# The 128-byte start of SBUF tiles in a channel-attention and Gelu feed-forward kernel

## The chip, the cores and the metric

One core of a Trainium2 chip runs the whole program. The metric is the device time of one execution in microseconds (us), the median of several executions. A time ending in ns is in nanoseconds.

## The reference, cut to what matters

```
q, k, v: (4, 6080, 256) float32; tau: a number; w_in: (256, 2048); w_out: (2048, 256)
qn = q / (norm(q over the 6080 rows) + 1e-6);  kn likewise
s  = kn^T @ qn / tau                 # 256 x 256 for each of the 4 batches
a  = softmax(s), each row divided by (its sum + 1e-9)
x  = v @ a                           # (24320, 256)
out = gelu(x @ w_in) @ w_out
```

## The kernel before, in words

Products are made in float32r, each operand split into a high part and a low remainder, so that one product is three matmuls (high by high, high by low, low by high). Attention is folded into the weights: for each batch the softmax matrix (`eh`, `el`) is multiplied into `w_in` by `w_group` (lines 341 to 364), which leaves the tiles `wh` and `wl`. The main loop then takes `v` in pairs of column blocks, 512 columns each (480 in the last of six pairs of a batch), and for each pair runs eight units. A unit is 7 first products (`product`, lines 416 to 418: weights `wh`/`wl`, moving operand `vh`/`vl`), Gelu on ScalarE (lines 424, 425), the split of its result (line 426), and 8 second products (lines 486 to 488: weights `wo`, moving operand `gh`/`gl`): 21 + 24 = 45 matmuls. There are 4 x 6 x 8 = 192 units.

Beside the units the next batch is prepared. `burst` (lines 177, 179) adds up its 256 x 256 score matrix out of `hl`: pairs of one 512-column matmul, whose moving operand is two runs of 256 columns, and one 256-column matmul. `norm_part` (lines 198, 199) loads `k` and `q` transposed and squares them on ScalarE, 24 activations a batch, each with its sum in a column of `nsum`. `softmax` (lines 264 to 335) is a generator of some stages: the sum of `nsum` (`nx`, line 281), its root on ScalarE (`ny`, 288), VectorE arithmetic (`nz`, `nr`, lines 291 to 294), `diag` and `rk` (297, 300), a matmul (303), the scaling and the row maximum (306, 309), the exponential with its sum in `den` (316), and `rden` (318, 319). Batch 0 does its part before the main loop with plain float32 matmuls (line 142), and its softmax stands alone on the way to the first unit.

A scheduler of the framework orders each engine's instructions: what is ready may be moved ahead of what was written earlier. A tile of a pool is used again only when the last instruction on its former holder is through; the pool `pm`, where all of the softmax's tiles lie, has one buffer for each name. A wait inside a tile goes by the slice that is read or written.

Tiles lie in SBUF one behind the other, pool by pool, each size rounded up to 32 bytes, at the same address in all partitions. In the kernel before the starts are, as remainders of 128 bytes:

| tiles | start mod 128 |
|---|---|
| `ident`, `ones`, `wh0` to `wh3`, `wl0` to `wl3` | 0 |
| `taut`, `rtau` (4 bytes each, the last of `const`) | 0, 32 |
| `win`, `wo`, `raw`, `hl`, `kqc`, `v_raw`, `vs`, `vh`, `vl`, `osb` | 64 |
| `junk`, `nx` | 64, 96 |
| `t0`, `t1` | 0 |
| `diag` | 96 |
| `e0`, `e1` | 64, 32 |
| `eh`, `el`, `sacc`, `nsum` (96 bytes) | 0 |
| `p1`, `p5`, `u2`, `h`, `gh`, `g`, `gl`, and in the first stage `raw0`, `acc`, `acc_p`, `sq` | 96 |

Of the kernel before, what the change touches and what calls it, by code (L numbers as in the profile page):

```python
# [9 lines left out]
F32 = mybir.dt.float32  # L10
F32R = mybir.dt.float32r
U32 = mybir.dt.uint32
AF = mybir.ActivationFunctionType
ALU = mybir.AluOpType
AX = mybir.AxisListType

P = 128
# [5 lines left out]
NCT = C // P  # L23
# [28 lines left out]
def channel_attention_gelu_ffn(ctx, tc, qk, kqt, vt, tau, w_in, w_out, out):  # L52
# [10 lines left out]
    nc = tc.nc  # L63
    const = ctx.enter_context(tc.tile_pool(name="const", bufs=1))
# [4 lines left out]
    pm = ctx.enter_context(tc.tile_pool(name="pm", bufs=1))  # L69
# [5 lines left out]
    def f32(ap):  # L75
        return ap.bitcast(F32)
# [6 lines left out]
    state = {}  # L83
# [10 lines left out]
    def bank():  # L94
        return ps_h.tile([P, NT], F32, name="ph")
# [4 lines left out]
    def load_first(js):  # L100
        if js % 3 == 2:
            raw = pqk.tile([P, JS, 2, C], F32, name="raw", bufs=3)
        else:
            raw = pst.tile([P, JS, 2, C], F32, name="raw0", bufs=4)
        step = 1 if js == 0 else JS
        for j in range(0, JS, step):
            nc.sync.dma_start(out=raw[:, j:j + step], in_=qk[0, :, js * JS + j:js * JS + j + step])
        raws[0, js] = raw
# [47 lines left out]
    def sum_up(nps, acc, start, stop):  # L156
        for i in range(2 * NCT):
            nc.tensor.matmul(nps[:, i:i + 1], acc[:, i // NCT, i % NCT * P:(i % NCT + 1) * P],
                             ones[:, 0:1], start=(start and i == 0), stop=stop, skip_group_check=True)
# [29 lines left out]
    NSC = -(-N // NS)  # L189

    def norm_part(b, i):

        t, c = divmod(i, NSC)
        n = min(NS, N - c * NS)
        if i == 0:
            state["nsum"] = pm.tile([P, 2 * NCT, NSC], F32, name="nsum")
        x = pqk.tile([P, NS], F32, name="kqc", bufs=2)
        nc.sync.dma_start(out=x[:, :n], in_=kqt[b, t, :, c * NS:c * NS + n])
        nc.scalar.activation(out=x[:, :n], in_=x[:, :n], func=AF.Square,  # L199
                             accum_out=state["nsum"][:, t, c:c + 1])  # L200
# [57 lines left out]

    def preload(func, after):

        junk = pm.tile([P, 2], F32, name="junk")
        nc.scalar.activation(out=junk, in_=after.bitcast(F32)[:, 0:2], func=func)

    def softmax(first, pool, name):
        x = pm.tile([P, 2 * NCT], F32, name="nx")
        ts = []
        for m in range(NCT):
            t = pm.tile([P, C], F32, name=f"t{m}")
            if first:
                nc.scalar.copy(out=t, in_=state["s"][m])  # L270
            else:
                s = state["sacc"]
                nc.vector.tensor_tensor(out=t, in0=s[:, m, 0:C], in1=s[:, m, C:2 * C], op=ALU.add)
            ts.append(t)
        if first:
            nps, acc = state.pop("nps"), state.pop("acc")
            for j in range(JS):
                sum_up(nps, acc[:, j], False, j == JS - 1)
            nc.vector.tensor_scalar(out=x, in0=nps[:, 0:2 * NCT], scalar1=1e-30, scalar2=None, op0=ALU.max)
        else:  # L280
            nc.vector.reduce_sum(out=x, in_=state["nsum"], axis=AX.X)
            nc.vector.tensor_scalar(out=x, in0=x, scalar1=1e-30, scalar2=None, op0=ALU.max)
        yield

        y = pm.tile([P, 2 * NCT], F32, name="ny")
        z = pm.tile([P, 2 * NCT], F32, name="nz")
        r = pm.tile([P, 2 * NCT], F32, name="nr")
        nc.scalar.activation(out=y, in_=x, func=AF.Sqrt)
        if first:
            preload(AF.Exp, y)  # L290
        nc.vector.reciprocal(out=z, in_=y)
        nc.vector.tensor_tensor(out=z, in0=z, in1=x, op=ALU.mult)
        nc.vector.scalar_tensor_tensor(out=z, in0=z, scalar=2e-6, in1=y, op0=ALU.add, op1=ALU.add)
        nc.vector.reciprocal(out=r, in_=z)

        diag = pm.tile([P, NCT, P], F32, name="diag")
        nc.vector.tensor_tensor(out=diag, in0=ident.unsqueeze(1).broadcast_to([P, NCT, P]),
                                in1=r[:, NCT:2 * NCT].unsqueeze(2).broadcast_to([P, NCT, P]), op=ALU.mult)
        rk = pm.tile([P, NCT], F32, name="rk")
        nc.vector.tensor_scalar(out=rk, in0=r[:, 0:NCT], scalar1=rtau, scalar2=4.0, op0=ALU.mult, op1=ALU.mult)  # L300
        yield
        rq = pool.tile([P, NT], F32, name=name)
        nc.tensor.matmul(rq[:, 0:C], ones, diag.rearrange("p h d -> p (h d)"), start=True, stop=True)
        nms = []
        for m in range(NCT):
            nc.vector.scalar_tensor_tensor(out=ts[m], in0=ts[m], scalar=rk[:, m:m + 1], in1=rq[:, 0:C],
                                           op0=ALU.mult, op1=ALU.mult)
            nm = pm.tile([P, 1], F32, name=f"nm{m}")
            nc.vector.reduce_max(out=nm, in_=ts[m], axis=AX.X, negate=True)
            nms.append(nm)  # L310
        yield
        es, rs = [], []
        for m in range(NCT):
            e = pm.tile([P, C], F32, name=f"e{m}")
            den = pm.tile([P, 1], F32, name=f"den{m}")
            nc.scalar.activation(out=e, in_=ts[m], func=AF.Exp, bias=nms[m], accum_out=den)
            rden = pm.tile([P, 1], F32, name=f"rden{m}", bufs=2)
            nc.vector.tensor_scalar(out=den, in0=den, scalar1=1e-9, scalar2=None, op0=ALU.add)
            nc.vector.reciprocal(out=rden, in_=den)
            es.append(e)  # L320
            rs.append(rden)
        yield
        tp = pool.tile([P, NT], F32, name=name)
        tpv = tp.rearrange("p (d c) -> p d c", d=NCT)
        for m in range(NCT):
            for d in range(NCT):
                nc.tensor.transpose(out=tpv[:, d, m * P:(m + 1) * P], in_=es[m][:, d * P:(d + 1) * P],
                                    identity=ident)
        eh = pm.tile([P, NCT, C], F32R, name="eh")
        el = pm.tile([P, NCT, C], F32R, name="el")  # L330
        marks["eh"] = nc.scalar.copy(out=eh, in_=tpv)
        if first:
            preload(AF.Gelu, eh[:, 0, 0:2])
        marks["el"] = nc.vector.tensor_tensor(out=el, in0=tpv, in1=f32(eh), op=ALU.subtract)
        state["e"], state["rden"] = (eh, el), rs


    whs = [const.tile([P, 7, 2, P], F32R, name=f"wh{g}") for g in range(NWG)]
# [2 lines left out]
    def w_group(b, g):  # L341

        eh, el = state["e"]
        win = wins.pop((b, g))
        tmp = pqk.tile([P, 8, 2, P], F32, name="hl")
        a21, a11, a22, a12 = (tmp[:, i] for i in range(4))
        s1, s2, s3, s4 = (tmp[:, 4 + i] for i in range(4))
        for m in range(NCT):
            cs = slice(m * P, (m + 1) * P)
            pwt = bank()  # L350
            for d in range(NCT):
                nc.tensor.matmul(pwt, eh[:, d, cs], win[:, 0, d], start=(d == 0), stop=False)  # L352
                nc.tensor.matmul(pwt, eh[:, d, cs], win[:, 1, d], start=False, stop=False)  # L353
                nc.tensor.matmul(pwt, el[:, d, cs], win[:, 0, d], start=False, stop=(d == NCT - 1))
            nc.scalar.activation(out=tmp[:, 2 * m:2 * m + 2], in_=pwt.rearrange("p (q r c) -> p r q c", q=2, r=2),
                                 func=AF.Copy, scale=state["rden"][m])
        tt = nc.vector.tensor_tensor
        tt(out=s1, in0=a21, in1=a22, op=ALU.add)
        tt(out=s3, in0=a11, in1=a21, op=ALU.subtract)
        tt(out=s2, in0=s1, in1=a11, op=ALU.subtract)  # L360
        tt(out=s4, in0=a12, in1=s2, op=ALU.subtract)
        for to, of in ((slice(0, 3), slice(1, 4)), (slice(3, 7), slice(4, 8))):
            nc.vector.tensor_copy(out=whs[g][:, to], in_=tmp[:, of])  # L363
            tt(out=wls[g][:, to], in0=tmp[:, of], in1=f32(whs[g][:, to]), op=ALU.subtract)  # L364
# [161 lines left out]
    preload(AF.Sqrt, ones)  # L526
    for js in range(AHEAD):
        load_first(js)
    taut = const.tile([P, 1], F32, name="taut")
    nc.sync.dma_start(out=taut, in_=tau)  # L530
    rtau = const.tile([P, 1], F32, name="rtau")
    nc.vector.reciprocal(out=rtau, in_=taut)

    units = [("in", 0, 0), ("in", 0, 1), ("out", 0, 0), ("in", 1, 0), ("in", 1, 1), ("out", 1, 0),
# [14 lines left out]
    with tc.high_priority():  # L549
        for _ in softmax(True, ps_o, "po"):  # L550
            pass
# [11 lines left out]
    def extras(b, p, u):  # L563
# [38 lines left out]
        if n0 <= w < n0 + 2 * NCT * NSC:  # L602
            norm_part(b + 1, w - n0)
# [59 lines left out]
```

## Time and profile before

| what | value |
|---|---|
| median of 3 runs | 2270.89 us (2270.64 to 2274.88) |
| the profiled execution's own time | 2270.88 us |
| its span, first to last instruction | 2269.1 us |
| mean granted clock of TensorE | 0.985 |
| TensorE matmuls busy (PE) | 2205.5 us |
| ScalarE (ACT) | 1444.4 us |
| VectorE (DVE) | 1425.4 us |
| GpSimd (POOL) | 82.8 us |

PE is TensorE's matmul row and PEld its weight loads, which overlap. Matmuls are pipelined and their ends are modelled, so the distance from one start to the next is read, not the duration. A few per cent of the matmul records can be missing. Lines are those of the kernel's source; the idle time before an instruction stands with what ended it.

### The profile page before, as it was taken

The numbers are of one execution on the slowest core, as the hardware profiler recorded it, in microseconds if no ns is written. First come the engines' busy times: TensorE is split into PE (matmuls) and PEld (weight loads), VectorE is DVE, ScalarE is ACT, GpSimd is POOL, SyncE is SP. The second block draws the span as 40 slices with busy tenths as digits, with TensorE's granted clock in tenths as the row PEclk, the third lists the DMA queues.
The fourth block names the chain that finished last, engine by engine and source line by source line (L and its number), as shares of the span: only waits on it lengthen the run. The fifth ranks groups of instructions, "written<-read, shape, count | busy, mean of one in ns | idle before, by whom it ended". The sixth has DMA issues, their size and how long they took to land.

```text
span 2269.1 us, 26295 instructions
## 1 busy us (share of the span) xinstructions
PE 2205.5 (97%) x9648; PEld 1799.1 (79%) x9648; DVE 1425.4 (63%) x2191; ACT 1444.4 (64%) x2616; POOL 82.8 (4%) x57
## 2 busy tenths in 40 slices
PE   6778999999999999999999999999999999999999
PEld 4556787888888888888888888888888888888887
DVE  6678675765667757657567666566566655555454
ACT  4567888765766656556666566566576666666565
POOL 5242000000000000000000000000000000000000
PEclk8789999999999999999999999999999999999999
DMA  7556777532224323323133333232222221221221
GB/s 255 180 185 214 247 265 235 174 101 84 84 102 138 121 66 121 109 78 120 48 115 129 107 103 115 89 103 81 77 83 84 83 93 47 92 85 48 91 68 53
DMA packets 76481, 265.03 MB, mean 117 GB/s; under 512 B 7616, under 2 KB 9664, under 8 KB 74304
## 3 DMA queue, kind: packets, MB, share of 16 engines
q1 hardware_dynamic: 76352, 263.35, 34.5%
q8 instruction: 76, 1.25, 0.2%
q14 instruction: 53, 0.43, 0.1%
HBM read 230.03 MB, written 33.29 MB: 116 GB/s over the span
## 4 chain that ended last, share of the span: by engine, by line
PE 85%; ACT 4%; DMA 4%; DVE 4%; POOL 1%; issue 1%; SPq 0%; ACTq 0%; POOLq 0%; DVEq 0%
PE po L488 14%; PE po L486 14%; PE po L487 14%; PE ph L416 12%; PE ph L417 12%; PE ph L418 12%; DMA kqc<-kqt 3%; PE ph L177 2%; ACT kqc L199 1%; PE ph L179 1%; DMA raw<-qk 1%; ACT g L425 1%; ACT gh L424 1%; PE ph L352 1%; PE ph L353 1%
## 5 line engine op out<-in xcount | busy, mean ns | idle before, releaser
L426 DVE TENSOR_TENSOR gl<-g,gh 128x512 fp32r<-128x512 f32 (+1 forms) x768 | 522.6, 683 | 151.7 <-ACT g L425 149.7
L488 PE MATMUL po<-gh,wo 128*128 128x512 f32 (+1 forms) x1536 | 606.0, 395 | 0.0
L487 PE MATMUL po<-gl,wo 128*128 128x512 f32 (+1 forms) x1536 | 599.9, 391 | 4.1 <-DVE gl L426 4.1
L486 PE MATMUL po<-gh,wo 128*128 128x512 f32 (+1 forms) x1536 | 601.2, 392 | 0.3 <-ACT gh L424 0.3
L441 DVE TENSOR_TENSOR h<-ph,p 128x512 f32<-128x512 f32 (+1 forms) x384 | 262.5, 684 | 534.0 <-PE ph L418 423.1
L424 ACT ACTIVATE gh<-h 128x512 fp32r<-128x512 f32 (+1 forms) x576 | 361.1, 627 | 296.7 <-DVE h L441 293.5
L416 PE MATMUL ph<-vh,wh 128*128 128x512 f32 (+1 forms) x1344 | 528.3, 393 | 18.9 <-DVE wh L363 13.9
L417 PE MATMUL ph<-vl,wh 128*128 128x512 f32 (+1 forms) x1344 | 528.4, 393 | 0.0
L418 PE MATMUL ph<-vh,wl 128*128 128x512 f32 (+1 forms) x1344 | 526.1, 393 | 2.0 <-DVE wl L364 2.0
L436 ACT COPY p<-ph 128x512 f32<-128x512 f32 (+1 forms) x384 | 222.8, 583 | 271.5 <-PE ph L418 271.1
L425 ACT ACTIVATE g<-h 128x512 f32<-128x512 f32 (+1 forms) x576 | 352.1, 611 | 0.0
L487 PEld LDWEIGHTS po<-gl,wo 128*128 128x128 f32 x1536 | 288.6, 188 | 68.3 <-DVE gl L426 6.1
L488 PEld LDWEIGHTS po<-gh,wo 128*128 128x128 f32 x1536 | 288.3, 188 | 65.7
L486 PEld LDWEIGHTS po<-gh,wo 128*128 128x128 f32 x1536 | 288.4, 188 | 63.8 <-ACT gh L424 1.2
L416 PEld LDWEIGHTS ph<-vh,wh 128*128 128x128 f32 x1344 | 253.9, 189 | 85.3 <-DVE wh L363 15.1
L417 PEld LDWEIGHTS ph<-vl,wh 128*128 128x128 f32 x1344 | 253.8, 189 | 57.0
L418 PEld LDWEIGHTS ph<-vh,wl 128*128 128x128 f32 x1344 | 254.1, 189 | 55.5 <-DVE wl L364 3.4
L436 ACT COPY u<-ph 128x512 f32<-128x512 f32 (+1 forms) x192 | 111.8, 582 | 121.3 <-PE ph L418 121.3
L441 DVE TENSOR_TENSOR h<-ph,u 128x512 f32<-128x512 f32 (+1 forms) x192 | 131.1, 683 | 3.5
L425 ACT ACTIVATE g<-ph 128x512 f32<-128x512 f32 (+1 forms) x192 | 112.0, 583 | 4.6 <-DVE gl L426 4.6
L424 ACT ACTIVATE gh<-ph 128x512 fp32r<-128x512 f32 (+1 forms) x192 | 110.4, 575 | 0.0
L177 PE MATMUL ph<-hl 128*128 128x512 f32 x288 | 101.8, 395 | 0.0
(107 smaller groups left out, 1424.0 us busy)
## 6 DMA issues: line engine op xcount, KB each, us to landing
wo<-keep_out SPq DMA_DIRECT2D x184, 512.0 KB, 3.3
raw<-qk SPq DMA_DIRECT2D x95, 512.0 KB, 4.2
kqc<-kqt SPq DMA_DIRECT2D x60, 512.0 KB, 4.5
v_raw<-vt SPq DMA_DIRECT2D x20, 1024.0 KB, 5.3
out<-osb SPq DMA_DIRECT2D x40, 512.0 KB, 3.3
win<-keep_in SPq DMA_DIRECT2D x12, 1024.0 KB, 4.8
kqc<-kqt SPq DMA_DIRECT2D x12, 480.0 KB, 4.5
raw<-w_in SPq DMA_DIRECT2D x8, 512.0 KB, 4.6
```

The lines of the kernel that those rows point to most:

```text
L177: nc.tensor.matmul(s, hl[:, 0, j, 0, cs], hl[:, :, j, 1], start=(i == 0), stop=False, skip_group_check=True)
L416: nc.tensor.matmul(ps[:, :n], wh, hi[:, :n], start=start, stop=False, skip_group_check=True)
L417: nc.tensor.matmul(ps[:, :n], wh, lo[:, :n], start=False, stop=False, skip_group_check=True)
L418: nc.tensor.matmul(ps[:, :n], wl, hi[:, :n], start=False, stop=stop, skip_group_check=True)
L424: nc.scalar.activation(out=gh[:, :n], in_=src, func=AF.Gelu)
L425: nc.scalar.activation(out=g[:, :n], in_=src, func=AF.Gelu)
L426: nc.vector.tensor_tensor(out=gl[:, :n], in0=g[:, :n], in1=f32(gh[:, :n]), op=ALU.subtract)
L436: nc.scalar.copy(out=t[:, :n], in_=ps[:, :n])
L441: nc.vector.tensor_tensor(out=h[:, :n], in0=ps[:, :n], in1=t[:, :n], op=ALU.add)
L486: nc.tensor.matmul(o, wo[:, 0, i, cs], gh[:, :n], start=first, stop=False)
L487: nc.tensor.matmul(o, wo[:, 0, i, cs], gl[:, :n], start=False, stop=False)
L488: nc.tensor.matmul(o, wo[:, 1, i, cs], gh[:, :n], start=False, stop=last)
```

## The change

Nothing is computed otherwise. Seven small tiles of the softmax (`nx`, `ny`, `nz`, `nr`, `rk`, `nm`, `den`) become slices of one tile `small` of 128 bytes a partition; the two `rden` become two columns of one 32-byte tile with two buffers; `taut` and `rtau` share a tile of 128 bytes; `nsum` has 8 columns of which 6 are used (128 bytes), and `junk` 16 of which 2 are used (64 bytes).

```
-            state["nsum"] = pm.tile([P, 2 * NCT, NSC], F32, name="nsum")
+            state["nsum"] = pm.tile([P, 2 * NCT, 8], F32, name="nsum")
...
-        junk = pm.tile([P, 2], F32, name="junk")
+        junk = pm.tile([P, 16], F32, name="junk")
...
     def softmax(first, pool, name):
-        x = pm.tile([P, 2 * NCT], F32, name="nx")
+        small = pm.tile([P, 32], F32, name="small")
+        x, y, z, r = (small[:, 4 * i:4 * i + 4] for i in range(4))
+        rk, nms, dens = (small[:, 16 + 2 * i:18 + 2 * i] for i in range(3))
...
-            nc.vector.reduce_sum(out=x, in_=state["nsum"], axis=AX.X)
+            nc.vector.reduce_sum(out=x, in_=state["nsum"][:, :, 0:NSC], axis=AX.X)
...
-        y = pm.tile([P, 2 * NCT], F32, name="ny")
-        z = pm.tile([P, 2 * NCT], F32, name="nz")
-        r = pm.tile([P, 2 * NCT], F32, name="nr")
...
-        rk = pm.tile([P, NCT], F32, name="rk")
...
-            nm = pm.tile([P, 1], F32, name=f"nm{m}")
-            nc.vector.reduce_max(out=nm, in_=ts[m], axis=AX.X, negate=True)
+            nc.vector.reduce_max(out=nms[:, m:m + 1], in_=ts[m], axis=AX.X, negate=True)
...
+        rden = pm.tile([P, 8], F32, name="rden", bufs=2)
         for m in range(NCT):
             e = pm.tile([P, C], F32, name=f"e{m}")
-            den = pm.tile([P, 1], F32, name=f"den{m}")
-            nc.scalar.activation(out=e, in_=ts[m], func=AF.Exp, bias=nms[m], accum_out=den)
-            rden = pm.tile([P, 1], F32, name=f"rden{m}", bufs=2)
+            den = dens[:, m:m + 1]
+            nc.scalar.activation(out=e, in_=ts[m], func=AF.Exp, bias=nms[:, m:m + 1], accum_out=den)
             nc.vector.tensor_scalar(out=den, in0=den, scalar1=1e-9, scalar2=None, op0=ALU.add)
-            nc.vector.reciprocal(out=rden, in_=den)
+            nc.vector.reciprocal(out=rden[:, m:m + 1], in_=den)
...
-    taut = const.tile([P, 1], F32, name="taut")
+    both = const.tile([P, 32], F32, name="taut")
+    taut = both[:, 0:1]
...
-    rtau = const.tile([P, 1], F32, name="rtau")
+    rtau = both[:, 8:9]
```

## Rows read from the trace of the kernel before

**Rows 1.** The page's busy time and share by engine; the chain's shares.

```profile
PE 2205.5 (97%) x9648; PEld 1799.1 (79%) x9648; DVE 1425.4 (63%) x2191; ACT 1444.4 (64%) x2616; POOL 82.8 (4%) x57
...
PE 85%; ACT 4%; DMA 4%; DVE 4%; POOL 1%; issue 1%; SPq 0%; ACTq 0%; POOLq 0%; DVEq 0%
```

**Rows 2.** Stretches: length, busy us of PE, PEld, DVE, ACT, POOL; clock, DMA share.

```profile
0.00:84.00 84.00, 55.25 (x212) 45.39 (x212) 55.09 (x58) 35.23 (x44) 39.47 (x29) 0.84 0.66 238
...
210.00:251.00 41.00, 41.00 (x182) 33.06 (x181) 30.79 (x49) 36.87 (x70) 0.00 (x0) 1.00 0.73 255
...
341.00:428.00 87.00, 86.08 (x380) 68.78 (x378) 55.70 (x87) 74.08 (x141) 0.00 (x0) 1.00 0.74 240
...
601.00:691.00 90.00, 90.00 (x413) 76.68 (x412) 58.73 (x99) 57.94 (x109) 0.00 (x0) 1.00 0.31 110
...
1815.80:2181.00 365.20, 365.20 (x1577) 295.38 (x1575) 196.51 (x304) 235.97 (x427) 0.00 (x0) 1.00 0.22 74
```

**Rows 3.** Line 416 in the last batch: duration, first and last start, 512 and 480 columns.

```profile
L416 PE MATMUL ph<-vh,wh x246: 380/388/501, 1815.8 to 2181.0; 128*128 128x512 f32 x123
...
L416 PE MATMUL ph<-vh,wh x43: 373/378/380, 2191.2 to 2250.0; 128*128 128x480 f32 x43
```

**Rows 4.** Timeline of TensorE in a burst: start, us; two of its pairs.

```profile
714.97 0.40 PE L177 MATMUL ph<-hl 128*128 128x512 f32 x1
...
717.05 0.40 PE L177 MATMUL ph<-hl 128*128 128x512 f32 x1
```

**Rows 5.** Line 142, plain float32: a run of 20 in the timeline; all of them.

```profile
13.75 4.48 PE L142 MATMUL ph<-raw 128*128 128x256 f32 x20
...
L142 PE MATMUL ph<-raw x192: 379/379/796, 3.5 to 83.5; 128*128 128x256 f32 x192
```

**Rows 6.** Groups by line and shape: count, busy us, mean ns, idle before.

```profile
L441 DVE TENSOR_TENSOR h<-ph,p 128x512 f32<-128x512 f32 x320 | 220.6, 689 | 452.9 <-PE ph L418 359.8 <-ACT gh L424 68.1 <-ACT osb L492 16.8
...
L187 DVE TENSOR_TENSOR sacc<-ph,sacc 128x512 f32<-128x512 f32 x66 | 45.4, 688 | 12.8 <-PE ph L179 12.6
...
L436 ACT COPY p<-ph 128x512 f32<-128x512 f32 x320 | 187.2, 588 | 246.0 <-PE ph L418 245.8
...
L331 ACT CAST eh<-ph 128x512 fp32r<-128x512 f32 x3 | 1.8, 587 | 0.8 <-PE ph L327 0.7
...
L487 PEld LDWEIGHTS po<-gl,wo 128*128 128x128 f32 x1536 | 288.6, 188 | 68.3 <-DVE gl L426 6.1
...
L418 PEld LDWEIGHTS ph<-vh,wl 128*128 128x128 f32 x1344 | 254.1, 189 | 55.5 <-DVE wl L364 3.4
```

**Rows 7.** Timeline around the first unit: start, us, engine, line, idle before.

```profile
98.64 0.55 DVE L363 CAST wh<-hl 128x768 fp32r<-128x768 f32 x1
...
99.24 0.50 PE L416 MATMUL ph<-vh,wh 128*128 128x512 f32 x1 [1.71 <-DVE wh L363]
...
101.24 0.68 DVE L363 CAST wh<-hl 128x1024 fp32r<-128x1024 f32 x1
```

**Rows 8.** Tiles `nsum`, `nr` and `den`: duration ns, first and last start us.

```profile
L281 DVE TENSOR_REDUCE nx<-nsum x3: 177/177/178, 249.7 to 426.1; 128x4 f32<-128x24 f32 x3
...
L294 DVE RECIPROCAL nr<-nz x4: 172/178/178, 86.2 to 596.6; 128x4 f32<-128x4 f32 x4
...
L300 DVE TENSOR_SCALAR rk<-nr,rtau x4: 217/218/223, 87.3 to 1136.6; 128x2 f32<-128x2 f32 x4
...
L319 DVE RECIPROCAL rden<-den x8: 140/152/156, 91.3 to 1681.4; 128x1 f32<-128x1 f32 x8
```

**Rows 9.** Squares of the last batch (340 to 430 us); the root's table loads.

```profile
L199 ACT ACTIVATE kqc<-kqc x24: 989/1060/1082, 342.2 to 424.9; 128x1024 f32<-128x1024 f32 x20, 128x960 f32<-128x960 f32 x4
L199 ACT ACTIVATION_READ_ACCUMULATOR kqc<-kqc x24: 183/188/211, 343.1 to 425.9; 128x1 f32 x24
...
L288 ACT ACT_TABLE_LOAD x3: 1283/1283/1283, 250.2 to 426.5; - x3
```

**Rows 10.** Waits: engine and line, waited for: us, times, longest.

```profile
PE ph L142 <- DMA raw<-qk: 28.6, 6, 10.5
```

More of the change, by code (lines that the diff above doesn't have):

```diff
@@ L259, in preload @@
     def preload(func, after):
-        junk = pm.tile([P, 2], F32, name="junk")
-        nc.scalar.activation(out=junk, in_=after.bitcast(F32)[:, 0:2], func=func)
+        junk = pm.tile([P, 16], F32, name="junk")
+        nc.scalar.activation(out=junk[:, 0:2], in_=after.bitcast(F32)[:, 0:2], func=func)
     def softmax(first, pool, name):
-        x = pm.tile([P, 2 * NCT], F32, name="nx")
+        small = pm.tile([P, 32], F32, name="small")
+        x, y, z, r = (small[:, 4 * i:4 * i + 4] for i in range(4))
+        rk, nms, dens = (small[:, 16 + 2 * i:18 + 2 * i] for i in range(3))
         ts = []
@@ L303, in softmax @@
         nc.tensor.matmul(rq[:, 0:C], ones, diag.rearrange("p h d -> p (h d)"), start=True, stop=True)
-        nms = []
         for m in range(NCT):
@@ L307, in softmax @@
                                            op0=ALU.mult, op1=ALU.mult)
-            nm = pm.tile([P, 1], F32, name=f"nm{m}")
-            nc.vector.reduce_max(out=nm, in_=ts[m], axis=AX.X, negate=True)
-            nms.append(nm)
+            nc.vector.reduce_max(out=nms[:, m:m + 1], in_=ts[m], axis=AX.X, negate=True)
         yield
-        es, rs = [], []
+        es = []
+        rden = pm.tile([P, 8], F32, name="rden", bufs=2)
         for m in range(NCT):
             e = pm.tile([P, C], F32, name=f"e{m}")
-            den = pm.tile([P, 1], F32, name=f"den{m}")
-            nc.scalar.activation(out=e, in_=ts[m], func=AF.Exp, bias=nms[m], accum_out=den)
-            rden = pm.tile([P, 1], F32, name=f"rden{m}", bufs=2)
+            den = dens[:, m:m + 1]
+            nc.scalar.activation(out=e, in_=ts[m], func=AF.Exp, bias=nms[:, m:m + 1], accum_out=den)
             nc.vector.tensor_scalar(out=den, in0=den, scalar1=1e-9, scalar2=None, op0=ALU.add)
-            nc.vector.reciprocal(out=rden, in_=den)
+            nc.vector.reciprocal(out=rden[:, m:m + 1], in_=den)
             es.append(e)
-            rs.append(rden)
         yield
@@ L334, in softmax @@
         marks["el"] = nc.vector.tensor_tensor(out=el, in0=tpv, in1=f32(eh), op=ALU.subtract)
-        state["e"], state["rden"] = (eh, el), rs
+        state["e"], state["rden"] = (eh, el), rden
     whs = [const.tile([P, 7, 2, P], F32R, name=f"wh{g}") for g in range(NWG)]
@@ L355, in w_group @@
             nc.scalar.activation(out=tmp[:, 2 * m:2 * m + 2], in_=pwt.rearrange("p (q r c) -> p r q c", q=2, r=2),
-                                 func=AF.Copy, scale=state["rden"][m])
+                                 func=AF.Copy, scale=state["rden"][:, m:m + 1])
         tt = nc.vector.tensor_tensor
```

## The prediction

> **What bounds the kernel now.** I read the page first, then stretches, then single streams. TensorE is busy 97% of the span and takes 85% of the chain that ended last [rows 1]. The stretches say where that holds: in the last batch PE is busy in all of 365.2 us at a clock of 1.00 (2.4 GHz), with ScalarE at 236 and VectorE at 197 us [rows 2]. There the time is the number of matmuls times the distance between their starts, and nothing else. Line 416 gives that distance: from 1815.8 to 2181.0 are 35 units of 45 matmuls, so 10.43 us a unit and 231.9 ns a 512-column matmul; from 2191.2 to 2250.0 are 6 units of 480 columns, 9.80 us and 217.8 ns [rows 3]. Only the start is different: up to 84 us PE is busy 55 us and waits for loads of `raw` (28.6 us in 6 waits) [rows 2, 10].
>
> So the change matters only if it alters those 232 ns, the start, or the order in which ScalarE and the queues do the preparing work.
>
> **Where the tiles go.** `const` grows by 64 bytes, so all from `win` to `osb` moves from remainder 64 to 0. In `pm`: `junk` 64 bytes, `small` 128, then `t0`, `t1`, `diag`, the two `rden` 64 together, and `e0` onward. That puts `e`, `eh`, `el`, `sacc`, `nsum` and the pool behind it (`gh`, `gl`, `h`, `g`, `raw0`) at 0; `t0`, `t1` and `diag`, behind 192 bytes, come to 64. That the change doesn't wholly do what it says is thus so, for three tiles that a softmax touches a few times; it is worth nothing.
>
> **VectorE, ScalarE and weight loads: 0.** The kernel before holds both sorts of tile, so the trace compares them itself [rows 6]. VectorE adds PSUM to a tile at 96 in 689 ns (`h`, line 441) and to one at 0 in 688 (`sacc`, line 187). ScalarE copies PSUM to 96 in 588 ns (`p`) and to 0 in 587 (`eh`). A weight load from `wo` at 64 takes 188 ns, from `wl` at 0 189. No engine but TensorE's moving stream can gain, and these are hidden behind it anyway.
>
> **TensorE's moving operand: 0 taken, bounds 0 and -148 us.** No float32r matmul before has its moving operand at 0 (`vh` 64, `gh` 96, `hl` 64), so no row shows this price. Plain float32 does 256 columns in two passes (192 records for 96 matmuls in the code) at (4.48 - 0.38)/19 = 215.8 ns a pass [rows 5], from tiles at 64 and 96; it reads a column half as fast. If a float32r matmul could run 512 columns in those 215.8 ns, 16.1 ns would go from each of 7,200 (115.9 us), 217.8 - 215.8 x 480/512 = 15.5 from each of 1,440 (22.3), 346.7 - 215.8 x 768/512 = 23 from each of the 288 pairs in bursts (6.6; a pair takes (717.05 - 714.97)/6 = 346.7 ns [rows 4]), 16.1 from 192 of the weight products (3.1): 148 us. That is the one end.
>
> What is the excess? If it were one extra line of 128 bytes per row that starts inside a line, it would be 32 columns at (10.43 - 9.80)/(45 x 32) = 0.44 ns, 14 ns, the same for 512 and 480. It is 16.1 and 15.5: this speaks for a price of the start. But a pair in a burst reads three such rows (two runs of 256 columns and one more) and should pay 42 ns; it pays 23, or 7.1% of its time at the clean rate, beside 7.5% and 7.7% for the other two. An excess that grows with the columns read is a rate, and a rate doesn't depend on where a row starts. I take 0, the end nearer to the burst's row; a loss I leave out of the sum, since no row with other remainders is slower.
>
> By the Trainium skill, "TensorE: Matmul & The Clock Gate" (Wait — 56ns, not 53.3ns?), warm matmuls follow each other every N/2.4 + 2.5 ns, measured there as 215.7 for 512; the float32 pass here agrees, the float32r stream (231.9) doesn't, and by that rule the kernel would come to an estimated 2123 us if the start were the whole cause. Against that, its page "SBUF — State Buffer" (Specifications) gives lines of 16 bytes; every tile before starts on a multiple of 32, so by it the sum is unchanged.
>
> **Waits inside the merged tile: 0.** Line 416 starts at 99.24 us, 50 ns after the first slice of `wh` (98.64 + 0.55) is written and 2 us ahead of the second (101.24) [rows 7]: waits go by slice, so `x`, `y`, `z` and the rest still wait only for each other. Were it by tile, the first softmax, which stands alone, would hold line 291 behind the preload's table load: such a load takes 1.28 us [rows 9], so the bound is about 1.5 us with its small activation.
>
> **The merged tile's one buffer: 0, from -1 to +10.** This moves work. Before, the sums of batches 2 and 3 are taken as soon as their squares are done: `nx` is written from 249.7 to 426.1 us, while `nr`, whose holder is read last by line 300, follows only at 596.6 [rows 8]. With one tile, `x` of batch 2 must wait until `den` of batch 1 is read (line 319, about 601 us), then `nsum` comes free, and then batch 3's 24 squares can be written. They leave 342 to 426 us: 24 x (1060 + 188) ns and one root's table load with the reload for Gelu, 30.0 + 2.6 us of ScalarE [rows 9], and 24 loads on SP's queue. SP's queue issues them then among `wo`, `raw` and `v_raw`, where the DMA engines are busy 0.31 of the time, against 0.74 in the old place [rows 2]. In that old place PE lost 0.9 us of 87 [rows 2], which is the gain. In the new one ScalarE has 57.9 of 90 us busy and PE loses nothing [rows 2]; the squares are due only in the next batch but one, so I spread them and take 0. The roots wait for nothing that PE needs soon.
>
> **Transfers at the start: 0, down to -3.** Rows of 4 KB now start on a multiple of 128. If each lost one of 17 pieces, the 0.66 x 84 = 55 us that the engines were busy up to 84 us [rows 2] would shrink by 3.3 us, part of it in the 28.6 us of waiting [rows 10]. Beside this stands the Trainium skill's "DMA: Bandwidth & Descriptors" (How a descriptor splits into AXI transactions): reads are cut at 256-byte boundaries. No run here shows it for writes to SBUF.
>
> **The sum.** The profiled execution took 2270.88 us, the median is 2270.89, so both give the same base: 2270.9 + 0 = 2271 us. A measurement of this kernel tells about 0.2%, 4.5 us, from no change.
>
> **The rivals.**
> 1. *The stream pays for its start* (faster, 0.20). For: the equal excess at 512 and 480 columns, and nothing else in a stretch that is TensorE alone. Against: the burst. With its 23 ns over three rows, 7.7 a row, it gives 8,640 x 7.7 + 288 x 23 + 192 x 7.7 = 75 us: 2196 us; the full excess gives 2123.
> 2. *The start and the early squares both gain* (faster, 0.07): -3.3 and -0.9, and a little of the later start-up: about 2264 us.
> 3. *The squares fall together at 601 to 691 us* (slower, 0.13). ScalarE would have 57.9 + 30.0 + 2.6 = 90.5 us to do there; the highest load at which PE lost nothing was 36.9 of 41, or 0.90 [rows 2]; 90.5/0.90 = 100.5, 10.5 us more, less 0.9: 2280 us. It decides from the point where ScalarE passes 0.90 x 90 = 81 us, that is when more than 16 squares fall there.
>
> **How the numbers follow.** Forecast 0.60, rivals 0.20, 0.07 and 0.13. Faster is 0.27, same 0.60, slower 0.13. The range takes in the forecast with the bounds of its small terms, the second rival and the third, and leaves out the first, 2 in 10: 2262 to 2281 us.
>
> **What would show it.** Right: units still of 10.42 us with 232 ns from start to start, line 441 and line 436 unchanged, `nx` last written after 1100 us instead of 426, and squares of batch 3 after 600 us. Wrong: a distance of 216 to 225 ns (first rival, and then everything in proportion), a first unit that starts well ahead of 99 us (second), or idle PE behind line 436 between 600 and 700 us (third). If `nx` is still written by 430 us, the step on the one buffer fell.

## The result, and the profile after

The changed kernel takes 2276.2 us (median of 20 runs, 2273.25 to 2280.72), the kernel before 2271.82 us on the same chip (20 runs, 2269.59 to 2276.54). The ratio is 1.0017 with an interval of [1.0010, 1.0024]: 4 us slower, by the ratio just under the 0.2% that counts here, though the interval reaches a little past it. The prediction was 2271.0 us, from 2262 to 2281, with "same" as the likeliest.

The profiled execution of the changed kernel took 2276.23 us, its span is 2274.4 us, the mean granted clock 0.986. Its lines stand five lower in most of the main loop: line 411 is line 416 of before, 413 is 418, 431 is 436, 436 is 441, 482 is 487. The page's busy time and its chain, as in [rows 1]:

```profile
PE 2208.2 (97%) x9648; PEld 1798.7 (79%) x9648; DVE 1428.2 (63%) x2191; ACT 1445.1 (64%) x2616; POOL 82.8 (4%) x57
...
PE 84%; ACT 6%; DMA 4%; DVE 4%; POOL 1%; issue 1%; SPq 0%; ACTq 0%; POOLq 0%; DVEq 0%
```

Nothing moved from one engine to another. ScalarE's share of the chain went from 4% to 6%, and the stretches show where. The columns are those of [rows 2]:

```profile
341.00:428.00 87.00, 87.00 (x388) 70.95 (x387) 58.42 (x85) 51.44 (x93) 0.00 (x0) 1.00 0.32 106
601.00:691.00 90.00, 85.93 (x389) 71.88 (x388) 55.92 (x97) 78.48 (x153) 0.00 (x0) 1.00 0.68 226
1815.80:2181.00 365.20, 365.20 (x1576) 295.37 (x1575) 195.13 (x300) 235.38 (x425) 0.00 (x0) 1.00 0.21 74
```

From 341 to 428 us ScalarE had 74.1 us to do before and has 51.4 now; from 601 to 691 us it had 57.9 and has 78.5, and there PE, which lost nothing before, stands idle for 90.00 - 85.93 = 4.1 us. The tiles say what moved. The columns are minimum, median and maximum duration in ns, then the first and the last start in us, as in [rows 8, 9]:

```profile
L284 DVE TENSOR_REDUCE small<-nsum x3: 171/171/178, 248.2 to 1149.5; 128x4 f32<-128x24 f32 x3
...
L199 ACT ACTIVATE kqc<-kqc x72: 990/1059/1107, 92.8 to 687.5; 128x1024 f32<-128x1024 f32 x60, 128x960 f32<-128x960 f32 x12
```

The last sum over `nsum` starts at 1149.5 us instead of 426.1, and the last square at 687.5 instead of 424.9. The waits in that stretch of the changed kernel (who waited for whom: us in all, times, the longest) show both sides of it:

```profile
ACT kqc L199 <- DMA kqc<-kqt: 7.2, 7, 2.4
...
PE ph L411 <- ACT u L431: 3.6, 2, 2.2
```

The squares wait for their own loads, and behind them come the copies of line 431 for which PE waits. It looks as if this were the whole loss of 4 us. It is not, as the experiments show. (Idle time by the windows is also a little short: a matmul counts as busy for its modelled 390 ns or so, but in an unbroken stream the next one starts after 232, so each wait shows shorter than it is.)

In the last batch, where PE never waits, line 411 can be set beside [rows 3]:

```profile
L411 PE MATMUL ph<-vh,wh x246: 394/394/502, 1815.9 to 2181.3; 128*128 128x512 f32 x123
```

35 units take 365.4 us where they took 365.2. But where bursts come in between, the distance is another. One row holds it: the 512-column matmuls of the last nine bursts, eight to a burst and a burst every three units, so that from the first start to the last are eight periods and the seven steps inside the last burst. First the kernel before, then the changed one:

```profile
L177 PE MATMUL ph<-hl x72: 392/395/402, 1356.9 to 1631.2; 128*128 128x512 f32 x72
```

```profile
L177 PE MATMUL ph<-hl x72: 393/396/403, 1360.6 to 1636.0; 128*128 128x512 f32 x72
```

With 0.35 us a step, as in [rows 4], a **period** is (274.3 - 2.45)/8 = 33.98 us before and (275.4 - 2.45)/8 = 34.12 us after (the rows round to 0.1, so about 0.02 either way). Four starts of one period show where the 0.14 us lie: the burst's first matmul, the first products that open the unit behind it and the next one, and the next burst. Again the kernel before, then the changed one:

```profile
1356.91 0.40 PE L177 MATMUL ph<-hl 128*128 128x512 f32 x1
...
1359.69 0.40 PE L416 MATMUL ph<-vh,wh 128*128 128x512 f32 x1
...
1370.05 0.39 PE L416 MATMUL ph<-vh,wh 128*128 128x512 f32 x1
...
1390.89 0.40 PE L177 MATMUL ph<-hl 128*128 128x512 f32 x1
```

```profile
1360.63 0.39 PE L177 MATMUL ph<-hl 128*128 128x512 f32 x1
...
1363.44 0.39 PE L411 MATMUL ph<-vh,wh 128*128 128x512 f32 x1
...
1373.89 0.40 PE L411 MATMUL ph<-vh,wh 128*128 128x512 f32 x1
...
1394.75 0.39 PE L177 MATMUL ph<-hl 128*128 128x512 f32 x1
```

The burst takes 2.78 us before and 2.81 after, the unit behind it 10.36 and 10.45, the two other units together 20.84 and 20.86. Most of the difference is that the first unit after a burst was quicker before. There are 36 bursts in a run (the twelve of the first batch come after two and three units in turn; there two units and a burst take 23.57 us before and 23.69 after): 36 x 0.13 to 0.14 = 4.7 to 5.0 us, as much as the whole loss. So two candidates of the same size stood against each other: 4.1 us of idle PE behind the crowded squares, and a slightly slower step of the matmuls.

### The profile page after: what moved, and what is told of

It reads as the page before. It is cut to its first block, busy times and chain, and to the rows that moved or that the text cites. A ratio compares the mean times of both kernels' runs of the same rounds, so it can differ in the third digit from the quotient of the medians.

```text
span 2274.4 us, 26299 instructions
## 1 busy us (share of the span) xinstructions
PE 2208.2 (97%) x9648; PEld 1798.7 (79%) x9648; DVE 1428.2 (63%) x2191; ACT 1445.1 (64%) x2616; POOL 82.8 (4%) x57
## 4 chain that ended last, share of the span: by engine, by line
PE 84%; ACT 6%; DMA 4%; DVE 4%; POOL 1%; issue 1%; SPq 0%; ACTq 0%; POOLq 0%; DVEq 0%
PE po L483 14%; PE po L482 14%; PE po L481 14%; PE ph L411 12%; PE ph L413 12%; PE ph L412 12%; DMA kqc<-kqt 3%; PE ph L177 3%; ACT kqc L199 2%; PE ph L179 1%; ACT g L420 1%; ACT gh L419 1%; DMA raw<-qk 1%; POOL hl L236 1%; DVE gl L421 0%
```

## The experiments

Every run is given with its ratio to the kernel before on the same chip. "Period" is worked out as above.

### The changed kernel once more

> The changed kernel again, beside the others on the same chip. Both theories: about 2276 us, 4 to 5 us above the kernel before (2271.8). The stretch from 601 to 691 us should again show PE idle for about 4 us.

Measured: 2275.49 us against 2272.34, ratio 1.0015 [1.0006, 1.0024]. The loss is there again: small, under the 0.2%, and with both intervals above 1 not nothing. The second half of the expectation missed. ScalarE has the squares in the same stretch, with 81.6 us even more to do than in the first profile, but PE stands idle there for only 0.9 us:

```profile
601.00:691.00 90.00, 89.10 (x403) 74.42 (x402) 58.70 (x104) 81.60 (x159) 0.00 (x0) 1.00 0.69 230
```

This execution took 2276.57 us, the one with 4.1 us of idle PE 2276.23. So the idle time of that stretch changes from one execution of the same program to the next, and the time of the whole does not follow it.

### The merged tile with three buffers

```
-        small = pm.tile([P, 32], F32, name="small")
+        small = pm.tile([P, 32], F32, name="small", bufs=3)
```

> The changed kernel with three buffers for the merged tile; all large tiles still start at 0 mod 128. Theory A (the one buffer moves the last batch's squares to 601 to 691 us, and nothing else costs): the sums of batches 2 and 3 are taken by 430 us again, PE loses about 1 us in 341 to 428 us and none in 601 to 691, time 2271.8 us within 1.5. Theory B (the new starts cost, in the matmul distance and the bursts): still about 2276 us. By the trace pieces of the changed kernel (start -1.2, slow gain of 3 us between 700 and 1770 us put down to addresses): about 2274 us.

Measured: 2276.61 us, 1.0020 [1.0011, 1.0028]. With three buffers the squares go back to their old place, and PE is busy in all of the disputed stretch:

```profile
601.00:691.00 90.00, 90.00 (x412) 76.65 (x411) 59.08 (x98) 58.40 (x110) 0.00 (x0) 1.00 0.31 108
```

The time doesn't fall (the profiled execution itself, at 2274.10 us, was the fastest of its eleven). The 4.1 us of idle PE were real in the profile and not what the change costs.

### The starts alone, and the merged tile alone

The two halves of the change can be had apart with pads. The starts alone: the kernel before with unused tiles, so that each large tile begins on a multiple of 128 bytes while every instruction keeps its place.

```
+    pm.tile([P, 16], F32, name="pad1")
     preload(AF.Sqrt, ones)
...
     rtau = const.tile([P, 1], F32, name="rtau")
+    const.tile([P, 16], F32, name="pad0")
...
-            state["nsum"] = pm.tile([P, 2 * NCT, NSC], F32, name="nsum")
+            state["nsum"] = pm.tile([P, 2 * NCT, 8], F32, name="nsum")
```

> The kernel before with three stretches of unused bytes, so that win to osb, h, gh, gl, p, u and raw0 start at 0 mod 128; no tile merged, every engine's order as before. Theory A: no difference, 2271.8 us within 1.5, the unit 10.42 us. Theory B: the 4 to 5 us of the change, about 2276 us. First rival of the prediction (a stream that pays for its start): 2196 us or less; the change's own result already speaks against it. By the trace pieces: a pair in a burst 352 ns instead of 347.7, +2 us in all.

The merged tile alone: `small` as in the change, and behind it a pad of 40 columns, so that the moving operands begin at 64 and 96 as before.

```
+        small = pm.tile([P, 32], F32, name="small")
+        x, y, z, r = (small[:, 4 * i:4 * i + 4] for i in range(4))
+        rk, nms, dens = (small[:, 16 + 2 * i:18 + 2 * i] for i in range(3))
...
+        if first:
+            pm.tile([P, 40], F32, name="pad")
```

> The kernel before with the seven small tiles merged into one of one buffer, and unused bytes so that all large tiles keep the remainders of the kernel before (64 and 96); every engine's order as in the changed kernel. Theory A: 2276 us, with PE idle for about 4 us in 601 to 691 us. Theory B: 2271.8 us. By the trace pieces: -2.3 us up to 600 us, +7 us from 602 to 685, so about 2276.5 us, and no drift of 3 us between 700 and 1770.

Measured: the starts alone 2276.14 us, 1.0017 [1.0008, 1.0025]; the merged tile alone 2271.37 us, 0.9993 [0.9984, 1.0002]. The bursts' rows, first of the starts alone, then of the merged tile alone:

```profile
L177 PE MATMUL ph<-hl x72: 393/397/403, 1361.4 to 1636.9; 128*128 128x512 f32 x72
```

```profile
L177 PE MATMUL ph<-hl x72: 392/395/402, 1358.6 to 1632.9; 128*128 128x512 f32 x72
```

275.5 us give a period of 34.13, 274.3 us one of 33.98. So the loss comes with the starts, while the instructions of every engine keep the old order, and none that can be measured comes with the merged tile. Its own stretches, merged tile alone:

```profile
341.00:428.00 87.00, 87.00 (x390) 71.18 (x389) 57.26 (x84) 50.69 (x93) 0.00 (x0) 1.00 0.33 114
601.00:691.00 90.00, 88.59 (x401) 74.11 (x400) 56.85 (x99) 80.03 (x155) 0.00 (x0) 1.00 0.68 226
691.00:780.00 89.00, 88.09 (x390) 71.58 (x389) 61.02 (x91) 53.30 (x96) 0.00 (x0) 1.00 0.35 118
```

The squares have moved, and PE loses 1.4 us of the later stretch and 0.9 of the one behind it, but the 0.9 us that it lost in the earlier one [rows 2] are back. Moving a crowd from one place to another changes where PE waits; in the sum no cost can be measured.

### Which start costs?

Three theories were set against each other: that the price hangs on the tiles in front (`win` to `osb`, among them `vh`, `vl` and `hl`), on those behind (`gh`, `gl`, `h`, `g`, `p`), or on whether the two groups have the same remainder. The pads are those of the run before in another choice: only the two pads of `pm` and `const` (front 0, behind 96), only `nsum` with 8 columns (front 64, behind 0), only `nsum` with 12 columns (both 64).

> The kernel before with unused bytes so that win, wo, raw, hl, kqc, vh, vl, osb start at 0 mod 128 (before 64); gh, gl, h, g, p, u, raw0 stay at 96; order as before. Read from the period of three units and one burst after 780 us, which is 33.99 us in the kernel before and 34.12 where all starts are 0. Theory V (the start of hl, vh or wo counts): 34.12 us and about 2276 us. Theory G (the start of gh and gl counts): 33.99 and 2272. Theory R (it costs when the streams of vh and gh have the same remainder): 33.99 and 2272.

> The kernel before with unused bytes so that gh, gl, h, g, p, u and raw0 start at 0 mod 128 (before 96); hl, vh, vl, wo and the rest stay at 64; order as before. Theory V: period 33.99 us, 2272 us. Theory G: 34.12 us, about 2276 us. Theory R: 33.99, 2272.

> The kernel before with unused bytes so that gh, gl, h, g, p, u and raw0 start at 64 mod 128 like hl, vh, vl and wo; order as before. Theory V: period 33.99 us, 2272 us. Theory G: where only a start at 0 costs, 33.99; where leaving 96 costs, 34.12. Theory R: 34.12 us, about 2276 us.

Measured: 2277.91 us, 1.0020 [1.0011, 1.0029]; 2275.54 us, 1.0014 [1.0006, 1.0023]; 2270.27 us, 0.9988 [0.9978, 0.9998]. The bursts' rows in the same order:

```profile
L177 PE MATMUL ph<-hl x72: 390/391/397, 1362.8 to 1638.4; 128*128 128x512 f32 x72
```

```profile
L177 PE MATMUL ph<-hl x72: 394/398/403, 1357.5 to 1632.9; 128*128 128x512 f32 x72
```

```profile
L177 PE MATMUL ph<-hl x72: 391/391/396, 1356.9 to 1631.4; 128*128 128x512 f32 x72
```

The periods are 34.14, 34.12 and 34.01 us. Either group moved to 0 costs the full amount by itself, and both together cost it once: none of the three theories holds as it stands. Two readings are left: a multiple of 128 is bad, or each layout simply has a step of its own.

### The squares spread

Since the squares of a next batch crowd ScalarE wherever they fall, they were spread: in the kernel before, each load and square is put behind the first Gelu of its unit.

```
-        nc.scalar.activation(out=gh[:, :n], in_=src, func=AF.Gelu)
+        marks["gelu"] = nc.scalar.activation(out=gh[:, :n], in_=src, func=AF.Gelu)
...
-            norm_part(b + 1, w - n0)
+            with behind("gelu"):
+                norm_part(b + 1, w - n0)
```

> The kernel before, its starts kept, with each of the 24 squares of a batch queued on ScalarE behind a Gelu of the unit it is written in, so that they come one a unit (from about the 8th unit of a batch) and not as early as their buffers allow. If crowded squares cost PE time: PE idle between 251 and 428 us falls from 2.2 us to under 0.5, the stretch 601 to 691 us stays full, and the time is 1 to 3 us below the kernel before, about 2270 us. If what PE loses there comes from other work or is won back later: no difference, 2272 us within 1.

Measured: 2265.68 us, 0.9967 [0.9955, 0.9979], 6.8 us below the kernel before on the same chip (2272.47) where 1 to 3 were expected. **This beats both kernels.** The squares now start from 234.0 to 1581.8 us, and the stretches that lost time are full:

```profile
251.00:341.00 90.00, 90.00 (x403) 73.59 (x402) 59.80 (x87) 61.15 (x112) 0.00 (x0) 1.00 0.46 148
341.00:428.00 87.00, 87.00 (x390) 71.18 (x389) 58.42 (x85) 58.29 (x107) 0.00 (x0) 1.00 0.45 150
```

ScalarE has 58 to 61 us there, where the kernel before had 74.1 of 87 in the second, and PE no longer waits there. The twelve bursts of the first batch show how much it is worth, first the kernel before, then this one:

```profile
L177 PE MATMUL ph<-hl x96: 387/395/403, 231.6 to 550.8; 128*128 128x512 f32 x96
```

```profile
L177 PE MATMUL ph<-hl x96: 392/395/402, 232.8 to 546.7; 128*128 128x512 f32 x96
```

From first to last they take 313.9 us instead of 319.2. The profiled execution (2268.05 us, with another the slowest of its seven) gives 2.5 of these 5.3 us back elsewhere, 1.2 of them ahead of the first burst. The loads of the squares move with them, and the runs don't separate the two; the waits of the kernel before from 251 to 780 us put 2.3 us of idle PE behind ScalarE's copies (line 436). The step of the matmuls has nothing to do with it: the bursts' row gives 274.4 us, a period of 33.99.

```profile
L177 PE MATMUL ph<-hl x72: 392/395/402, 1352.9 to 1627.3; 128*128 128x512 f32 x72
```

### Do the two add, and is 0 special?

> The changed kernel with the ten pairs of squares of each next batch set behind the first GELU of each work item, as in e7_squares_spread. If the start of the tiles and the place of the squares are two separate costs, they add: e7 stood at 0.9967 of the kernel before, the starts alone at 1.0017, so 0.9984, about 2268 to 2270 us, and a period of three units and one burst of 34.12 us after 780 us. If the late squares of the changed kernel were part of its loss, the spread takes that too and it comes nearer to e7: 0.997 or less, about 2265 us.

> e7_squares_spread with 4 columns more in the sums tile, so that every large tile begins at 64 past a multiple of 128 bytes, as in e6_all_starts_at_64. If both gains stand by themselves: 0.9967 times 0.9988, about 0.9955, 2261 to 2264 us, period 34.02 us. If the small gain of e6 was only the batch norms' stage falling well, nothing is added to e7: about 2265 to 2267 us.

> The kernel before with two pads, so that every large tile begins at 96 past a multiple of 128 bytes. If only a start at a multiple of 128 bytes costs something: the period stays at 33.99 to 34.02 us and the time at about 2270 to 2272 us. If each set of starts simply has a sequence of distances of its own: a period of its own, anywhere from 33.9 to 34.2 us, and a time of 2267 to 2277 us. If equal starts of the two groups of tiles were what costs: 34.12 us and 2276 us, as with all starts at 0.

The last one has a pad of 24 columns in `pm` and one of 8 in `const`, in the places shown above. Measured: the changed kernel with the squares spread 2270.81 us, 0.9989 [0.9980, 0.9997]; spread with all starts at 64 2265.01 us, 0.9965 [0.9951, 0.9979]; all starts at 96 2288.75 us, 1.0067 [1.0054, 1.0079]. The first adds as expected: 0.9984 was worked out and lies in the interval, the time is 0.8 us above the range given, and its bursts (1355.7 to 1631.1 us) give a period of 34.12. The starts cost the same, as far as can be measured, whatever the squares do. (Its expectation speaks of ten pairs of squares; the edit spreads all 24, as before.) The second is no better than the spread alone, so the small gain of all starts at 64 does not stand by itself; its bursts' row (274.6 us, a period of 34.02) shows no quicker step either:

```profile
L177 PE MATMUL ph<-hl x72: 391/391/396, 1351.6 to 1626.2; 128*128 128x512 f32 x72
```

The third lies beyond all three of its ranges, in period and time, and rules out that only a start at a multiple of 128 costs. The bursts' row of all starts at 96, and the first products of its last batch:

```profile
L177 PE MATMUL ph<-hl x72: 392/398/403, 1368.2 to 1645.7; 128*128 128x512 f32 x72
```

```profile
L416 PE MATMUL ph<-vh,wh x246: 381/397/499, 1831.4 to 2199.4; 128*128 128x512 f32 x123
```

277.5 us for the nine bursts give a period of 34.38 us, and 35 units take 368.0 us instead of 365.2: 2.8/35 = 0.08 us a unit. About 36 x 0.40 = 14.4 us for the periods with bursts and 40 x 0.08 = 3.2 for the last batch's units of 512 columns are 17.6 us; the spans of the two profiled executions differ by 18.2 (2287.3 - 2269.1), the medians by 15.5 (2288.75 - 2273.21). A layout in which neither group of tiles starts at a multiple of 128 costs four times as much as the changed one. Of the two readings the second is left: each of the six sets of starts has its own step.

## Why the prediction was right, and where it was wrong

It was right in the whole: 2276.2 us lies in the range, and the change is inside 0.2%. Some of that is luck: the 4 us come from a term that the sum had at nothing, and the upper end of the range was there for the third rival, which is not what cost them. Step by step:

**What bounds the kernel**: right. Only the matmuls' step and the preparing work mattered; the largest shift of the time came from the step.

**VectorE, ScalarE and weight loads, 0**: right. The groups by shape of the changed kernel, beside [rows 6]: `h` now begins at 0 instead of 96, and so does `p`.

```profile
L436 DVE TENSOR_TENSOR h<-ph,p 128x512 f32<-128x512 f32 x320 | 220.6, 689 | 458.8 <-PE ph L413 363.6 <-ACT gh L419 72.3 <-ACT osb L487 16.7
...
L431 ACT COPY p<-ph 128x512 f32<-128x512 f32 x320 | 187.6, 588 | 265.6 <-PE ph L413 265.2
...
L482 PEld LDWEIGHTS po<-gl,wo 128*128 128x128 f32 x1536 | 289.0, 188 | 71.0 <-DVE gl L421 6.1
```

689, 588 and 188 ns, to the nanosecond as before.

**TensorE's moving operand, 0 taken, bounds 0 and -148**: this step was off, by its size and by its upper bound. The reasoning that ruled out the -148 holds: the 232 ns are not the price of a start inside a line, and with all starts on lines the units of the last batch still take 365.4/35 = 10.44 us. The prediction went on: "a loss I leave out of the sum, since no row with other remainders is slower". Here is the loss, about +4 us by the starts alone (0.17% of 2272). No row of before could show the other layouts, because a kernel has one. But a bound above nothing was to be had from the trace: in the kernel before the units between two bursts, 45 like matmuls each, take 10.36, 10.42 and 10.42 us, so the step is no constant of the matmul, and 0.06 us in each of 192 units are an estimated 11 us. The 4 us of the change lie inside that, the 15 of all starts at 96 do not. The burst's 7.1%, beside 7.5 and 7.7, was no real difference: rows that are rounded to 0.01 us leave it anywhere from 6.6 to 7.6%, and all eight pairs of a burst together (2.78 us) come to 7.4. The argument from the three rows of a pair stands without it, since eight pairs at 42 ns more than the clean rate would take 2.93 us.

**Waits inside the merged tile, 0**: right. In the first softmax line 291 starts with the preload's table load and not behind it:

```profile
84.14 1.28 ACT L262 ACT_TABLE_LOAD   x1
...
84.16 0.18 DVE L291 RECIPROCAL small<-small 128x4 f32<-128x4 f32 x1 [0.27 <-ACT small L288]
```

The first unit starts at 98.15 us in the changed kernel, against 99.24:

```profile
98.15 0.50 PE L411 MATMUL ph<-vh,wh 128*128 128x512 f32 x1 [1.71 <-DVE wh L358]
```

That it is earlier is no gain: in the run of the changed kernel once more it starts at 99.57 us.

**The merged tile's one buffer, 0, from -1 to +10**: the mechanism came as described, to the sums at 1149.5 us and the squares at 601 to 688 us. "I spread them and take 0" was wrong in the first half: they did fall together. The 0 holds all the same, since the merged tile alone stands at 0.9993 [0.9984, 1.0002].

**The third rival** thus had its place right and its price wrong. It was to decide from 81 us of ScalarE in 90; ScalarE came to 78.5, under the point, and PE idled 4.1 us even so, 3.6 of them behind the copies (line 431, before 436) that the prediction had named as the sign. Before, PE lost 0.9 us at 74.1 of 87 [rows 2], which is 0.85, and the changed kernel's second profile lost only 0.9 at 81.6 of 90: the highest load in a stretch without loss was no threshold, since a mean over 90 us doesn't say how long one copy of line 431 stands behind squares that have come together. In the first profile part of the price came back in the stretches that the squares had left: from 251 to 515 us PE idles 0.5 us instead of 2.6, where the prediction put the gain at 0.9. What the crowds of all batches, with their loads, cost in their old places is seen in the run with the squares spread: 0.33%, 7 us.

**Transfers at the start, 0 down to -3**: right, no gain is to be seen. PE waited 29.4 us for `raw`, against 28.6 [rows 10], and 27.9 in the changed kernel once more:

```profile
PE ph L142 <- DMA raw<-qk: 29.4, 7, 10.8
```

**The first rival** (2196 us) and the second (2264 us) didn't come: the units of the last batch are no shorter, and the first unit starts 1.1 us earlier in one profile and 0.3 later in the other, which is not the start that the second needed (3.3).

What stays open is why the starts set the step. Two layouts with all starts alike but at 0 and 96, and the instructions in the same order, differ by 0.5%, and no wait, clock (1.00 in every stretch of the main loop shown) or engine in the profile accounts for it. Which access pays is open too: each group holds more than one kind of tile, the one in front the weights `wo` beside the moving operands `vh` and `hl`. Nor is it shown that the remainder of 128, and not of another number, is what counts; by the tiles' sizes the tiles behind lie 256 bytes further on in the starts alone than in the changed kernel, and the period is the same. Other remainders, 32 among them, were not tried.

## What to carry to other kernels

Whoever changes a tile's size, its count or the order in which tiles are made shifts every tile behind it, and in a kernel bound by TensorE this alone is worth some tenths of a per cent in either direction: before a difference of that size is put down to the change, run the old code with pads that give the new starts, and the new code with pads that keep the old ones. Round addresses are no goal in themselves; a layout is to be measured. Idle time of the bounding engine in one stretch is not yet a loss of the whole: profile the same program twice, look for the stretch that got it back, and if work that is ready early crowds an engine wherever it falls, spread it over the units, as the versions did that beat both kernels by the most.

## What the runs showed of the hardware

The step of this kernel's float32r matmuls of 512 columns depends on where the program's tiles begin, and goes by a sequence that repeats to the nanosecond or two. From start to start, between 1360 and 1396 us, where three first and three second products alternate (ns, as worked out from the starts in the trace; the remainders of 128 bytes of the tiles in front and behind stand ahead):

```
64, 96 (before)    225 229 231   232 227 236   = 1380
 0,  0 (changed)   232 232 233   232 232 233   = 1394
96, 96             235 235 235   234 229 235   = 1403
                   235 243 238   236 228 230   = 1410, in turn with the line above
```

After two groups of second products in a row, which come once a unit, the kernel before leaves this sequence for 20 to 30 matmuls at 224 to 242 ns. In the last batch it does so in every unit and comes out at the 10.43 us of the changed kernel; after a burst it is back in the quick sequence within a few matmuls, and that is the larger part of what its periods with bursts have ahead (0.09 of 0.14 us in the period shown above). The periods of the six layouts: 64 and 96, 33.98 us; 64 and 64, 34.01; 0 and 0, 34.12; 64 and 0, 34.12; 0 and 96, 34.14; 96 and 96, 34.38. The Trainium skill, "SBUF — State Buffer" (Specifications), gives SBUF lines of 16 bytes. From that the prediction reasoned that starts which are all multiples of 32, as these are, are alike; the page itself doesn't say so, and the 15 us of all starts at 96 show that they are not. VectorE, ScalarE and the weight loads took the same time to the nanosecond or two with starts behind at 0 and at 96.
